# A two-layer decode kernel: norms in two products, queries turned in PSUM, the gate worked ahead, one more V head kept, K slots freed by halves

## The chip, the cores and the metric

The kernel runs on one core of a Trainium2 chip. Its time is the device time of one execution in microseconds (us), the median of several runs. Smaller is better.

## The reference, cut to what matters

Four sequences (B = 4) decode one token each. The same block, attention and then a gated feed-forward net, is applied twice with the same weights and the same K and V caches:

```python
B, Sq, D = 4, 1, 512;  Hq, Hkv, Sk, Dh = 32, 8, 4096, 128;  F = 1792   # all bf16
x = x + _A_ref(_layernorm(x), A_k_cache, A_v_cache, A_wq, A_wo)
x = x + _B_ref(_layernorm(x), B_w_gate, B_w_up, B_w_down)
x = x + _A_ref(_layernorm(x), A_k_cache, A_v_cache, A_wq, A_wo)
x = x + _B_ref(_layernorm(x), B_w_gate, B_w_up, B_w_down)
# _A_ref: q = x @ wq;  softmax(q k^T / sqrt(128)) v, 4 query heads to a K/V head;  @ wo
# _B_ref: (gelu(x @ w_gate) * (x @ w_up)) @ w_down
```

One head of K or V of one sequence is 4096 x 128 bf16, 1 MiB; the whole K cache is 32 MiB, the V cache 32 MiB, and the weights are 13.25 MiB. The kernel keeps twelve head-sized slots beside the weights; what is not kept for the second pass is read twice.

## The kernel before, in words

**Tiling and stages.** Below, L is the pass: 0 for the first application of attention, 1 for the second. Sequences are taken one after the other. For sequence b the kernel loads its 8 K heads and keeps them for both passes, computes the scores of pass 0, streams the V heads of pass 0, goes through the dense chain (output projection, norm, feed-forward, norm, query projection), computes the scores of pass 1 on the K heads still there, and streams the V heads again for pass 1. The pass-1 V loads of sequence b come after the K and pass-0 V loads of sequence b + 1. At the end one output projection, norm and feed-forward for all four sequences, and the output.

**Slots.** `KV` has 12 slots of 1 MiB (`SLOTS`); the four quarters of `wq_sb` serve as four more once the last query projection is done (`extra`, line 994). A slot has two halves, and a load takes a slot (`ld_head`, line 348, issued on line 351) or, for the V loads named in `HALVES`, half a slot (`ld_part`, line 354, issued on line 357). V head 7 of sequences 1, 2 and 3 is loaded once and kept for pass 1 (`HELD`); that of sequence 0 is loaded twice. A K head gives both halves of its slot free when the pass-1 scores of its group of four heads are complete (`loads_k`, line 753).

**Loads.** All loads go through SyncE's queue in one fixed order (`pl.load`, lines 804 to 818): x, wq, K of sequence 0, half of wo, V, the other half of wo, the gate, up and down weights (the down weights in two loads of 7 chunks, line 798), then K(1), V(1) pass 0, V(0) pass 1, K(2), and so on. A load that waits for its slot holds up all loads behind it.

**Order of the other work.** `Plan` (line 64) holds a node for each step with an assumed duration; `run` (line 108) goes through them with assumed costs and priorities (`LEAD`, `PATIENCE`) and writes down one order, in which each engine then executes. `warm` (line 215) puts spare matmuls, whose results nobody reads, into TensorE's planned gaps (`spin`, line 1002, executed on line 1004).

**Scores.** `scores(b, z, m)` (line 401): group z of four K heads, half m of each head's keys, 16 matmuls of 512 columns (line 415). K heads other than 5 and 7 are first transposed in place by VectorE in two halves (`turn`, line 363, executed on line 366); heads 5 and 7 go through TensorE (line 373) and ScalarE (line 379).

**The dense chain.** `outproj` (line 878): the first groups of heads with `proj` (line 613), out of PSUM in two halves (line 632), summed by a matmul (line 639), the last groups straight to their place with `proj_last` (line 623); then `addback` (transpose on line 646, add on line 647). `ln` (line 821): square (line 500), one product with ones for sums and squares together (line 506), reduction and centring (lines 512 and 513), variance (lines 521 and 522), and ScalarE's root (lines 529 and 530) beside what follows. The feed-forward: gate and up products (`up`, line 655), the gate's transpose (`ffturn`, line 662), the polynomial of gelu (lines 678 to 681), the exponential on ScalarE (line 688), then the up product's transpose (line 662 again), its product with the gate (lines 695 to 699), division (lines 705 to 707), and the down product in two steps (line 715). `qproj` (line 829): for each half z of the query heads 16 matmuls (line 538), ScalarE takes them out of PSUM (line 551), VectorE transposes (line 556), `qsplit` masks (line 595), a small matmul (line 605) and `expand` (line 392) spread the queries for the scores.

**The end.** After the last V half: scale (line 493), `proj_last`, `addback`, the rows of x for the residual (lines 727 and 728), norm, feed-forward, sum (line 732), output (line 735).

## Time and profile before

| | |
|---|---|
| median of 3 runs | 292.3 us (291.77 to 293.2) |
| the profiled execution's own time | 291.89 us |
| its span in the profile | 290.1 us |
| time around the span (start and end) | 1.8 us |
| granted TensorE clock | 0.998 |
| loads: K 32 of 1 MiB; V 38 of 1 MiB (4 of them into `wq_sb`) and 46 of 512 KiB | 93 MiB |
| read from HBM | 111.42 MB |

In the profile, PE is TensorE's matmul, PEld its weight load, DVE VectorE, ACT ScalarE, SP SyncE with the loads' queue. "L351" is line 351 of the kernel. A line of the chain of waits or of the timeline begins with its start and its length in us. In a table by stretches the columns are the stretch, its length, the busy time and count of each engine, the granted clock, the busy share of the 16 DMA engines (it can read over 1), and the GB/s moved.

### The profile page before, as it was taken

How to read it: one execution, taken by the hardware profiler on the slowest of the kernel's cores; microseconds unless marked ns; L12 is line 12 of the kernel's file. 1: busy time of each engine (PE TensorE's matmuls, PEld its weight loads, DVE VectorE, ACT ScalarE, POOL GpSimd, SP SyncE). 2: the span in 40 equal slices, each digit the busy share in tenths (PEclk: the TensorE clock that was granted, in tenths of full speed). 3: DMA queues.
4: the chain of work that ended last, by engine and by line, in shares of the span. 5: the costliest groups of instructions: out<-in, count | busy, mean ns of one | idle time of the engine just before them, and what ended most of it. 6: DMA issues, size and time to landing. Idle time of an engine off the chain costs nothing.

```text
span 290.1 us, 9733 instructions
## 1 busy us (share of the span) xinstructions
PE 236.3 (81%) x4419; PEld 138.3 (48%) x4419; DVE 133.5 (46%) x380; ACT 74.5 (26%) x167; POOL 0.7 (0%) x6
## 2 busy tenths in 40 slices
PE   4988887878687888798888698879977889897794
PEld 1433454443233565455434465554445655565552
DVE  4149911002289942052389721343998213444034
ACT  1020751001023852101224731000338321113010
POOL 0000000000000000000000000000000000000000
PEclk9999999999999999999999999999999999999999
DMA  7999999999999999999999999999999999999910
GB/s 312 412 421 419 376 405 416 414 371 426 415 407 395 419 421 417 402 407 406 393 417 416 425 416 411 405 407 390 413 422 416 408 387 403 396 382 420 411 47 1
DMA packets 21657, 112.04 MB, mean 386 GB/s; under 512 B 2032, under 2 KB 6128, under 8 KB 12272
## 3 DMA queue, kind: packets, MB, share of 16 engines
q1 hardware_dynamic: 21568, 111.42, 95.3%
q8 instruction: 34, 0.56, 0.8%
q14 instruction: 7, 0.06, 0.0%
q10 hardware_dynamic: 48, 0.01, 0.0%
HBM read 111.42 MB, written 0.00 MB: 384 GB/s over the span
## 4 chain that ended last, share of the span: by engine, by line
DMA 62%; PE 16%; SPq 11%; DVE 7%; issue 2%; ACT 1%; DVEq 0%
DMA KV<-in_A_v_cache_dram 43%; DMA KV<-in_A_k_cache_dram 8%; SPq L351 7%; PE O_ps L485 7%; DMA wd_sb<-in_B_w_down_dram 6%; DMA wq_sb<-in_A_v_cache_dram 5%; SPq L741 3%; PE S_ps L415 3%; DVE KV L366 2%; PE R_ps L715 1%; PE R_ps L538 1%; DVE PA L662 1%; PE S_ps L1004 1%; PE R_ps L655 1%; DVE sm L421 1%
## 5 line engine op out<-in xcount | busy, mean ns | idle before, releaser
L485 PE MATMUL O_ps<-PA,KV 128*128 128x56 bf16 x1920 | 66.3, 188 | 20.8 <-DMA KV<-in_A_v_cache_dram 17.3
L485 PEld LDWEIGHTS <-KV 128*128 128x128 bf16 x1920 | 57.6, 97 | 40.8 <-DMA KV<-in_A_v_cache_dram 32.4
L1004 PE MATMUL S_ps<-iden_b 128*128 128x512 bf16 x226 | 67.7, 401 | 3.6 <-DVE iden_b L321 3.6
L366 DVE STREAM_TRANSPOSE KV<-KV 128x1024 int32<-128x1024 int32 x48 | 56.5, 1214 | 0.6 <-DMA KV<-in_A_k_cache_dram 0.4
L379 ACT ACTIVATE KV<-R_ps 128x512 bf16<-128x512 f32 x64 | 34.9, 595 | 28.0 <-PE R_ps L373 27.9
L415 PE MATMUL S_ps<-KV,PA 128*32 128x512 bf16 x384 | 35.3, 394 | 2.1 <-DVE KV L366 1.3
L1004 PEld LDWEIGHTS <-iden_b 128*128 128x128 bf16 x227 | 21.9, 107 | 27.6 <-issue 11.7
L373 PE MATMUL R_ps<-iden_b,KV 128*128 128x128 bf16 x256 | 22.1, 219 | 6.3 <-ACT KV L379 3.1
L421 DVE TENSOR_REDUCE sm<-S_ps 128x1 f32<-128x512 f32 x16 | 10.8, 677 | 27.4 <-PE S_ps L415 27.4
L373 PEld LDWEIGHTS <-KV 128*128 128x128 bf16 x256 | 15.8, 97 | 14.8 <-issue 10.2
L415 PEld LDWEIGHTS <-PA 128*32 128x32 bf16 x384 | 11.4, 94 | 13.2 <-issue 4.4
L493 DVE TENSOR_TENSOR OT<-O_ps,XS 128x4 bf16<-128x4 f32 (+1 forms) x12 | 2.0, 164 | 32.9 <-PE O_ps L485 32.9
L415 PE MATMUL S_ps<-KV,QN 128*32 128x512 bf16 x128 | 16.8, 381 | 0.2 <-ACT KV L379 0.2
L438 ACT ACTIVATE PA<-S_ps,sm 128x512 bf16<-128x512 f32 x16 | 11.7, 732 | 20.4 <-DVE sm L432 17.6
L632 ACT ACTIVATE PA<-R_ps 128x256 f32<-128x256 f32 x10 | 3.8, 384 | 46.2 <-PE R_ps L613 41.1
L529 ACT ACTIVATE sm<-sm 128x1 f32<-128x1 f32 (+1 forms) x10 | 2.0, 203 | 52.6 <-DVE sm L522 52.6
L493 DVE TENSOR_TENSOR OT<-O_ps,rdk 128x16 bf16<-128x16 f32 (+3 forms) x18 | 3.1, 170 | 26.7 <-PE O_ps L485 26.7
L463 ACT ACTIVATE PA<-T_ps 128x512 bf16<-128x512 f32 x16 | 9.6, 597 | 13.0 <-PE T_ps L455 11.8
L556 DVE STREAM_TRANSPOSE PA<-PA 128x256 int32<-128x256 int32 x10 | 4.4, 437 | 14.9 <-ACT PA L551 14.2
L613 PE MATMUL R_ps<-wo_sb,OT 128*1 128x512 bf16 (+1 forms) x124 | 8.7, 378 | 2.6 <-DMA wo_sb<-in_A_wo_dram 1.4
L646 DVE STREAM_TRANSPOSE PA<-R_ps 128x128 f32<-128x128 f32 x9 | 2.9, 317 | 16.5 <-PE R_ps L623 10.2
L447 DVE STREAM_TRANSPOSE PA<-PA 128x256 int32<-128x256 int32 x16 | 7.0, 434 | 7.5 <-ACT PA L438 7.5
(92 smaller groups left out, 173.9 us busy)
## 6 DMA issues: line engine op xcount, KB each, us to landing
KV<-in_A_v_cache_dram SPq DMA_DIRECT2D x34, 1024.0 KB, 15.0
KV<-in_A_k_cache_dram SPq DMA_DIRECT2D x32, 1024.0 KB, 13.5
KV<-in_A_v_cache_dram SPq DMA_DIRECT2D x46, 512.0 KB, 7.0
wq_sb<-in_A_wq_dram SPq DMA_DIRECT2D x1, 4096.0 KB, 12.2
wo_sb<-in_A_wo_dram SPq DMA_DIRECT2D x2, 2048.0 KB, 19.5
wq_sb<-in_A_v_cache_dram SPq DMA_DIRECT2D x4, 1024.0 KB
wg_sb<-in_B_w_gate_dram SPq DMA_DIRECT2D x1, 1792.0 KB
wu_sb<-in_B_w_up_dram SPq DMA_DIRECT2D x1, 1792.0 KB
```

The lines of the kernel that those rows point to most:

```text
L351: nc.sync.dma_start(out=where[name], in_=src.rearrange("(p c) d -> p (c d)", p=P))
L366: nc.vector.transpose(out=w, in_=w)
L373: nc.tensor.matmul(R_ps[k % 2][:, P * u:P * u + P], lhsT=where[name][:, at:at + P], rhs=iden_b[:], start=True, stop=True)
L379: nc.scalar.activation(out=where[name][:, 512 * k:512 * k + 512], in_=R_ps[k % 2][:], func=ACT.Copy)
L415: nc.tensor.matmul(S_ps[z][32 * t:32 * t + 32], lhsT=w, rhs=k, start=(m == 0 and x == 0), stop=(m == 1 and x == 3))
L421: nc.vector.tensor_reduce(out=cms[:, z:z + 1], in_=S_ps[z][:].rearrange("p c r -> p (c r)"), axis=AX.X, op=ALU.max)
L438: nc.scalar.activation(out=PW[L][z].rearrange("p (a r e) -> p a r e", a=8, e=2), in_=S_ps[z][:].rearrange("p (a e) r -> p a r e", e=2), fu ...
L463: nc.scalar.activation(out=PW[L][z], in_=T_ps[z][:].rearrange("p t x -> p (t x)"), func=ACT.Copy)
L485: nc.tensor.matmul(Ov[L][:, j], lhsT=vw[:, c, :], rhs=w[:, c // 2, :, c % 2].unsqueeze(1).broadcast_to([P, WIDE, 4]), start=(m == 0 and c ...
L613: nc.tensor.matmul(R_ps[0][32 * i:32 * i + nb, :], lhsT=src[:, 4 * j + i, 0:nb], rhs=wo_sb[:, 4 * j + i, :], start=(first and j == heads[0 ...
L741: return lambda pick: nc.sync.dma_start(out=dst, in_=src.rearrange(pat, q=P))
L1004: nc.tensor.matmul(sinks[place].rearrange("p (a n) -> p a n", a=4), lhsT=iden_b[:], rhs=every, start=True, stop=True)
```

## The change

- The sums and the squares of a norm become two products. The first no longer waits for the squares; the second goes to another PSUM place and feeds only the variance.
- For the first half of the query heads of the dense chains (not for the first query projection), the 16 matmuls leave the queries in an order in which VectorE transposes them within PSUM; ScalarE's way out is gone there. The second half stays.
- In the feed-forward the gate's branch (exponential, division) is worked through before the up product is transposed. That transpose and the last product are cut in two (8 and 6 chunks), the down weights' loads and the down product likewise. At the end, the rows' transpose for the residual goes behind the norm.
- V head 7 of sequence 0 is kept for pass 1 too; its two half loads go.
- A K slot is given free in two halves, each after its own half of the pass-1 scores. K head 3 of sequence 1 comes in two loads of half a slot, the second into the other half of the first one's slot.
- In the last projection heads 4 and 5 are scaled and projected apart.
- The planner's assumed durations and priorities change (`LEAD`, `PATIENCE`, `WARM`, `FILL`, the sizes given to `pl.load`), and with them the order on each engine. The spare matmuls go from 227 to 263.

```diff
-HELD = ((), (7,), (7,), (7,))
-HALVES = {(b, 1, j) for b in range(3) for j in range(8)} | {(3, 1, 6)}
+HELD = ((7,), (7,), (7,), (7,))
+HALVES = {(b, 1, j) for b in range(3) for j in range(7)} | {(3, 1, 6)}
+HALF_HELD = (None, None, None, None)
+K_HALVES = {(1, 3)}
...
-DMA_FETCH = 1.5
+DMA_FETCH = 0.8
...
-WARM = 0.45
-FILL = 0.7
+WARM = 0.55
+FILL = 0.9
...
+    CUT = (0, 8, CF)
...
+    def ln_place(s, nb):
+        return O_ps[0][:, 512 - CD * nb:] if s else R_ps[1][:, 0:CD * nb]
+
-    def ln_mm(bs, nb):
+    def ln_mm(s, bs, nb):
         def emit():
-            st = R_ps[1][:, 0:2 * CD * nb].rearrange("p (s k b) -> p s k b", s=2, k=CD)
-            nc.tensor.matmul(st, lhsT=ones_mean, rhs=XS[:, :, :, bs], start=True, stop=True)
+            st = ln_place(s, nb).rearrange("p (k b) -> p k b", k=CD)
+            nc.tensor.matmul(st, lhsT=ones_mean, rhs=XS[:, s, :, bs], start=True, stop=True)
...
+    def qmm_apart(bs):
+        def emit():
+            for c in range(CD):
+                w = wq_sb[:, c, :].rearrange("q (z g h j k e) -> q z g h j e k", z=2, g=2, h=8, j=2, e=2)
+                for jg in range(4):
+                    nc.tensor.matmul(R_ps[0][32 * jg:32 * jg + 1, :].rearrange("p (h e k) -> p h e k", h=8, e=2),
+                                     lhsT=xn[:, c, bs], rhs=w[:, 0, jg % 2, :, jg // 2],
+                                     start=(c == 0), stop=(c == CD - 1))
+        return emit
+
+    def qturn_apart():
+        nc.vector.transpose(out=R_ps[0][:], in_=R_ps[0][:])
...
-            pl.load(("k", b, j), 8, ld_head(("k", b, j), A_k_cache[b, j]), [("sc", b, 1, j // 4, 1)],
-                    soft=soft)
+            name, src = ("k", b, j), A_k_cache[b, j]
+            rd = [[("sc", b, 1, j // 4, m)] for m in range(2)]
+            if (b, j) in K_HALVES:
+                for m in range(2):
+                    if j >= 3:
+                        soft = [("sc", b - 1, 1, 0 if j < 7 else 1, m)]
+                    pl.load(name + (m,), 4.15, ld_part(name, m, src), rd[m], soft=soft, half=True)
+            else:
+                pl.load(name, 8, ld_head(name, src), rd, soft=soft)
...
     def ln(tag, after, bs, nb, y, by=1.0):
-        a = add(("lnq", tag), "DVE", 0.17, [after], ln_sq(bs, nb))
-        a = add(("lnm", tag), "PE", 0.4, [a], ln_mm(bs, nb), ins=4)
-        a = add(("lnc", tag), "DVE", 0.37, [a], ln_mid(bs, nb))
-        v = add(("lnv", tag), "DVE", 0.33, [a], ln_var(nb))
+        s = add(("lnq", tag), "DVE", 0.17, [after], ln_sq(bs, nb))
+        m = add(("lnm", tag), "PE", 0.35, [after], ln_mm(0, bs, nb), ins=4)
+        a = add(("lnc", tag), "DVE", 0.3, [m], ln_mid(bs, nb))
+        s = add(("lns", tag), "PE", 0.35, [s, m], ln_mm(1, bs, nb), ins=4)
+        v = add(("lnv", tag), "DVE", 0.45, [s, a], ln_var(nb))
...
+            if not z and not root:
+                after = add(("qm", tag, z), "PE", 1.1, [after], qmm_apart(bs), ins=32)
+                last = add(("qt", tag, z), "DVE", 0.72, [after], qturn_apart)
+                last = spread_q(b, 1, z, last, "apart")
+                continue
...
+    def ffn(tag, a, bs, nb, y, clear=None):
+        one = nb == 1
+        g = [None, None]
+        for z, w in ((0, wg_sb), (1, wu_sb)):
+            g[z] = add(("up", tag, z), "PE", 0.93, [a, g[0], "wu" if z else "wg"], up(z, w, bs, nb), ins=32)
+        t0 = add(("ft", tag, 0), "DVE", 0.65, [g[0]], ffturn(0))
+        a = add(("ga", tag), "DVE", 0.59 if one else 0.72, [t0, ("lnr", ("f", tag))], gelu_a(nb, y))
+        e = add(("gb", tag), "ACT", 0.22 if one else 0.25, [a], gelu_b(nb))
+        if not one:
+            a = add(("gz", tag), "DVE", 0.28, [a], gelu_z(nb, y))
+        e = add(("gd", tag), "DVE", 0.72 if one else 0.95, [e, a], gelu_d(nb, y))
+        t1, h, n = a, None, None
+        for k in range(2):
+            t1 = add(("ft", tag, 1 + k), "DVE", (0.44, 0.36)[k], [g[1], t1], ffturn(1, k))
+            h = add(("gh", tag, k), "DVE", 0.18, [t1, e, h], gelu_h(nb, k))
+            if k and clear:
+                add(("zz", tag), "DVE", 0.07, [h], clear)
+            n = add(("dn", tag, k), "PE", (0.55, 0.42)[k], [h, n, ("wd", k)], down(nb, k), ins=8 * (CUT[k + 1] - CUT[k]))
+        return n
```

More of the change, by code (lines that the diff above doesn't have):

```diff
@@ L607, in qrep, with proj @@
         return emit
-    def proj(src, nb, heads, first, last):
+    def proj(src, cols, nb, heads, first, last):
         def emit():
@@ L616, in proj, with proj_last @@
         return emit
-    def proj_last(src, nb, heads, last):
+    def proj_last(src, cols, nb, heads, last):
         def emit():
@@ L876, in parts, with outproj @@
         return [(h, [("os", b, 1, i)]) for i, h in enumerate(g)]
-    def outproj(tag, b, L, bs, nb, after):
-        pre, p = None, parts(b, L)
-        whole = len(p) - (1 if L else 2)
+    def outproj(tag, p, whole, L, bs, nb, after, free):
+        pre, cols = None, bs if L else slice(0, 1)
         for k, (heads, deps) in enumerate(p[:whole]):
             pre = add(tag + (k,), "PE", 0.21 * len(heads) + 0.15, deps + [pre] + after,
-                      proj(OT[L], nb, heads, k == 0, k == whole - 1), ins=8 * len(heads))
-        free = [("val", b, 0, j, 1) for j in range(4)]
+                      proj(OT[L], cols, nb, heads, k == 0, k == whole - 1), ins=8 * len(heads))
         for m in range(2):
```

169 lines of the change are left out of this document (84 added, 85 removed).

## The prediction

> **What bounds the kernel now.** I read the page's second, third and fourth parts first, then tables by stretches.
>
> ```profile
> span 290.1 us, 9733 instructions
> DMA  7999999999999999999999999999999999999910
> q1 hardware_dynamic: 21568, 111.42, 95.3%
> DMA 62%; PE 16%; SPq 11%; DVE 7%; issue 2%; ACT 1%; DVEq 0%
> ```
>
> The transfers are busy from the first slices to the last but two. 111.42 MB leave in one queue, and 62% of the chain that ended last is DMA. So bytes set the time, together with the moments in which the queue has nothing to do, and the end, where no transfer is left. The stretches give the speed and those moments; the last column is GB/s.
>
> ```profile
> 84.00:90.00 6.00, 4.93 (x84) 2.52 (x87) 5.57 (x15) 1.49 (x5) 0.00 (x0) 1.00 0.93 377
> 100.00:110.00 10.00, 8.31 (x180) 6.06 (x178) 4.59 (x9) 5.82 (x12) 0.00 (x0) 1.00 1.02 419
> 120.00:130.00 10.00, 9.22 (x228) 5.95 (x227) 4.14 (x19) 1.00 (x4) 0.00 (x0) 1.00 1.02 405
> 140.00:146.00 6.00, 4.97 (x99) 2.62 (x97) 3.35 (x9) 1.53 (x4) 0.00 (x0) 1.00 0.99 385
> 196.00:202.00 6.00, 5.51 (x117) 3.14 (x113) 1.33 (x4) 0.60 (x1) 0.00 (x0) 1.00 1.02 387
> 230.00:236.00 6.00, 5.27 (x128) 3.54 (x120) 2.16 (x8) 1.38 (x3) 0.00 (x0) 1.00 0.98 380
> 248.00:258.00 10.00, 8.57 (x207) 5.00 (x207) 3.27 (x17) 1.60 (x4) 0.00 (x0) 1.00 1.02 372
> ```
>
> Whole-slot loads run at 419 GB/s (100 to 110), half-slot loads at 405 (120 to 130). Against 419, the stretch 84 to 90 loses (419 - 377) / 419 x 6 = 0.60 us; the four later ones lose 0.49, 0.46, 0.56 and 1.12, together 2.63. These are the places where loads wait for slots.
>
> **The change, part by part.**
>
> *One MiB less: -2.5.* V head 7 of sequence 0 isn't loaded again. 1.0486 MB at 405 GB/s are 2.59 us; K head 3 of sequence 1, loaded by halves now, goes from 2.50 (at 419) to 2.59. The net is -2.50.
>
> At this place the Trainium skill speaks against the split: "DMA: Bandwidth & Descriptors", sections on the anatomy of one DMA and on bandwidth, gives each DMA a fixed 2.0 us beside its bytes and asks for at least 1 MiB. By it, an estimate, K head 3 in two loads costs 2.0 us more than in one, and the sum would be -1.1. The 405 against 419 disagrees with that for loads in a filled queue.
>
> *The slot that the kept head holds: +1.1.* After the down weights, the queue has had the first four K heads of sequence 1 in the slots that V of pass 0 left; the rest wait for the pass-1 scores to free K slots. The kept head leaves three such slots. The chain of waits, and the timeline, show how far the scores are:
>
> ```profile
> 61.10 17.76 DMA wd_sb<-in_B_w_down_dram
> 78.90 0.59 PE R_ps L715 x28
> 80.07 0.18 DVE XS L500
> 80.29 0.40 PE R_ps L506 x2
> 81.16 1.04 PE R_ps L538 x16
> 82.22 0.61 ACT PA L551
> 82.85 0.46 DVE PA L556
> 83.33 0.27 DVE qs L595
> ```
>
> ```profile
> 81.38 1.25 DVE L366 STREAM_TRANSPOSE KV<-KV 128x1024 int32<-128x1024 int32 x1
> 84.39 2.02 PE L415 MATMUL S_ps<-KV,PA 128*32 128x512 bf16 x32 [0.21 <-DVE PA L392]
> 86.42 3.08 SPq L351 DMA_DIRECT2D KV<-in_A_k_cache_dram  x4
> ```
>
> The weights land at 78.86, and the next K load goes out at 86.42, right behind the 32 score matmuls. With three heads the queue is empty 2.50 us sooner. Against that, the first half of a slot is free after 16 of the 32, 1.0 sooner. The chain itself: 24 instead of 28 down matmuls save 4/28 x 0.59 = 0.08, the square (80.07 to 80.29) leaves the path, 0.22, and ScalarE's way out with the transpose behind it (82.22 to 83.31, 1.09) gives place to one transpose in PSUM.
>
> That transpose is new. Between the rows that are nearest, from PSUM:
>
> ```profile
> L662 DVE STREAM_TRANSPOSE PA<-R_ps 128x448 f32<-128x448 f32 x10 | 6.5, 648 | 7.2 <-PE R_ps L655 7.1
> L646 DVE STREAM_TRANSPOSE PA<-R_ps 128x128 f32<-128x128 f32 x9 | 2.9, 317 | 16.5 <-PE R_ps L623 10.2 <-PE R_ps L715 6.3
> L333 DVE MEMSET O_ps<- 128x512 f32 x2 | 1.0, 485 | 0.1
> ```
>
> a column costs (648 - 317) / 320 = 1.03 ns, so 512 cost 0.71 us. The floor is 0.65 (the 448-column row); the ceiling, with all of a 512-column PSUM write on top, 1.20. I take 0.71, for the shape and the source are the same. That would gain 0.38. But in the changed order of VectorE's instructions a K head's transpose of 1.25 (line 366, from 81.38 before) now stands directly ahead of it, and ends at about 82.6. The query turn then ends at 82.6 + 0.71 = 83.3, where it ended before: the chain of sequence 0 gains nothing. So the first half slot is asked for 1.0 sooner and the queue is empty 2.50 sooner. If all engines ran dry together, this would add 1.5; in 84 to 90 the queue still moved 377 of 419, so they run dry one by one. I take +1.1, between 0.3 (the last engine hardly waits) and 2.5 (the halves don't help).
>
> *The chains of sequences 1 to 3: -1.3.* There the square and the query turn do gain, 0.22 twice and 0.38, for no K transpose stands before them; and the new order puts the chain ahead: the pass-1 scores of group 0 stand before the last V head's two halves, where they stood between and behind them. In the chain of waits before:
>
> ```profile
> 140.77 0.60 PE O_ps L485 x16
> 141.38 1.13 PE S_ps L415 x16
> ```
>
> the last V half's 16 matmuls come first and the scores end at 142.5; this is in the stretch that loses 0.49. The K load that is third in the queue now goes into a K slot freed by these scores. Of the 2.63 us lost in the four later stretches I take back half, 1.3: most of the first two (0.95), whose place this is, a third of the others. The bounds are -2.6 (all) and 0.
>
> *The end: -0.4.* From the timeline of the last 12 us:
>
> ```profile
> 278.41 0.39 PE L639 MATMUL R_ps<-PA,sm 128*4 128x128 f32 x4
> 278.73 0.61 PE L485 MATMUL O_ps<-PA,KV 128*128 128x56 bf16 x16
> 280.68 0.17 DVE L500 TENSOR_TENSOR XS<-XS 128x16 f32<-128x16 f32 x1
> 280.90 0.41 PE L506 MATMUL R_ps<-XS,sm 128*128 128x32 f32 x2 [0.59 <-DVE XS L500]
> 280.97 0.41 DVE L728 STREAM_TRANSPOSE PA<-PA 128x128 f32<-128x128 f32 x1
> 284.05 0.22 DVE L681 SCALAR_TENSOR_TENSOR PA<-PA 128x56 f32<-128x56 f32 x1
> 284.30 0.25 ACT L688 ACTIVATE PA<-PA 128x56 f32<-128x56 f32 x1 [1.80 <-DVE PA L681]
> 285.31 0.50 DVE L706 RECIPROCAL PA<-PA 128x56 f32<-128x56 f32 x1
> 286.12 0.95 PE L715 MATMUL R_ps<-wd_sb,PA 128*4 128x128 bf16 x56 [1.01 <-DVE PA L707]
> 287.12 0.29 DVE L732 TENSOR_TENSOR PA<-PA,R_ps 128x128 bf16<-128x128 f32 x1 [1.06 <-PE R_ps L715]
> 287.48 0.68 SPq L735 DMA_DIRECT2D out_dram<-PA  x2
> ```
>
> The last V half's product waits at 278.73 behind a sum of line 639, which the new order puts earlier: -0.2, between 0 and the sum's 0.39. The norm's product starts at 280.68 instead of 280.90: -0.22. The rows' transpose of 0.41 moves to the wait for the gate product (0.96), which hides it; without that cover it would cost its 0.41. The gate's branch gains nothing here, worked through from the gelu's end (284.26): a multiplication 0.24, eight chunks' transpose 0.45 by the slope above, sum and minimum 0.12, reciprocal 0.52, product 0.23, product 0.2, then 32 matmuls beside six chunks' transpose 0.38 and a product 0.2, then 24 matmuls, 0.42: 2.8, as from 284.26 to 287.07 before. Bounds for the end: -0.9 (the second transpose wholly hidden) and 0.
>
> *At nothing:* 36 more spare matmuls (they stand in gaps), the strided query weights (the scores' matmuls of line 415 read their K heads strided too, 16 in 1.13 us as line 538 has 16 in 1.04), and the masked queries read from PSUM, under 0.1 in a chain that isn't at the end. If a gap is shorter than planned, a spare matmul of 0.22 delays what stands behind it, and the V halves with it; that is in the third rival.
>
> *Sum:* -2.5 + 1.1 - 1.3 - 0.4 = -3.1. The profiled execution (291.89, of which 1.8 lie around the span) would come to 288.8; it lies 0.4 below the median of the runs shown, and the forecast for the median is 292.3 - 3.1 = **289.2**.
>
> **The rivals.**
>
> 1. *The gap takes the MiB.* For it: VectorE's K transpose ahead of the query turn. If the first half slot goes out no sooner than 86.42, the whole 2.5 is lost after 84, and if the chains then win nothing either, the end alone is left: 292.3 - 0.4 = 291.9. Against it: half a slot is free after 16 of 32 score matmuls, whatever the chain does. 0.14.
> 2. *All the lost time comes back.* -2.6 instead of -1.3, +0.3 instead of +1.1, -0.9 at the end: 292.3 - 5.7 = 286.6. For it: the stretches lose only while loads wait. Against it: in 120 to 130 loads by halves move 405 with no wait in sight. 0.12.
> 3. *The chain blocks the V halves (slower).* TensorE works in order. With norm, query product (0.41 + 0.4 + 1.04 = 1.9 us) and scores ahead of V halves that have landed, their half slots are given back that much later. If three chains each cost 1.9, the time is 292.3 - 2.5 + 1.1 + 5.7 - 0.4 = 296.2. It decides by more than 0.5% from (1.46 + 2.5 - 1.1 + 0.4) / 3 = 1.1 us each. For it: 248 to 258 before, where chain and halves mix, is the worst stretch, 1.12. Against it: three slots of halves are 7.8 us of transfers in hand. 0.09.
> 4. *A small load into an empty queue pays its way alone.* From the output's issue (287.48) to the span's end (290.1) there are 2.6 us for 1 KB; one such way more, at the gap, gives 289.2 + 2.6 = 291.8. The skill's fixed 2.0 says the same with its own figure. Against it: 405 against 419. 0.02.
>
> **How the numbers follow.** The forecast's own case, 288.0 to 290.8, has 0.63; the rivals 0.14, 0.12, 0.09 and 0.02. A measurement of this kernel tells about 0.5% from no change, 1.46 us: faster is below 290.84, slower above 293.76. Faster: 0.63 + 0.12 = 0.75. Same: 0.14 + 0.02 = 0.16. Slower: 0.09. From 287.0 to 291.9 the range leaves out the slower case and about half of the second rival, some 0.15 to 0.17.
>
> **What would show it.** The queue's bytes fall by 1.05 MB. The stretch 84 to 90 moves less than 377 GB/s, with the first half-slot K load at about 85.5; a load at 84.7 would say that the K transpose wasn't in the way, one at 86.4 the first rival. The dips around 140 and 196 (moved by what was won until then) rise towards 405; if they are deeper, the third rival is at work. At the end, the norm's product follows the add-back at once, and from the gelu's end to the last matmul it is still 2.8 us. The forecast is wrong if the gap costs over 2 us or if the V halves' products wait for TensorE and not for DMA.

## The result, and the profile after

The changed kernel takes 295.1 us (292.43 to 295.79, 7 runs) beside 292.8 us (median of 7) of the kernel before on the same chip: ratio 1.0068, 95% interval 1.0038 to 1.0097. It is 0.68% slower, 2.0 us, where 289.2 us, 3.1 less than before, was forecast. All times below are compared as ratios to the kernel before, measured beside each kernel on the same chip. A ratio is formed from the executions in the faster of two states alone (one of before, 298.56 us, was in the slower), so it isn't the quotient of the medians. The profiled execution took 295.61 us, 0.5 above its median, with a span of 293.8. That is 3.7 above the span of before, more than the ratio's 2.0: part of what the two traces differ in is the spread between executions.

The page of the changed kernel, the lines that answer to those of before:

```profile
span 293.8 us, 9878 instructions
PEclk9999999999999999999997999999999999979999
DMA  7999999999979999999999999999999999999800
q1 hardware_dynamic: 21424, 110.37, 93.8%
DMA 45%; PE 32%; DVE 9%; ACT 5%; SPq 4%; issue 4%; DVEq 0%; ACTq 0%
```

The bytes fell by 1.05 MB as they should, and yet DMA's share of the chain fell from 62% to 45%: TensorE's rose from 16% to 32%, "issue" from 2% to 4%. The kernel was a stream of loads with TensorE beside it; in this execution the two take turns in setting the time. The clock row has a 7 in two places; by the trace these are two windows of 3.4 us at half speed, at 154.9 and 257.3. The profiled execution of before had none ahead of its last 1.1 us, but the kernel before isn't free of them: its other executions have mean granted clocks of 0.968 to 1.0.

The same seven stretches as before (last column GB/s):

```profile
84.00:90.00 6.00, 5.27 (x91) 2.88 (x90) 5.24 (x13) 1.25 (x4) 0.00 (x0) 1.00 0.66 221
100.00:110.00 10.00, 7.23 (x149) 5.35 (x147) 5.63 (x12) 6.75 (x14) 0.00 (x0) 1.00 1.01 418
120.00:130.00 10.00, 8.77 (x213) 5.63 (x213) 2.76 (x15) 1.17 (x4) 0.00 (x0) 1.00 1.01 402
140.00:146.00 6.00, 5.53 (x107) 2.81 (x106) 2.60 (x11) 1.42 (x4) 0.00 (x0) 1.00 1.00 378
196.00:202.00 6.00, 5.30 (x134) 3.63 (x134) 1.12 (x2) 0.00 (x0) 0.00 (x0) 1.00 0.97 337
230.00:236.00 6.00, 5.86 (x133) 3.78 (x132) 2.15 (x8) 2.10 (x5) 0.00 (x0) 1.00 1.01 414
248.00:258.00 10.00, 7.43 (x202) 5.40 (x201) 4.96 (x23) 0.81 (x2) 0.00 (x0) 0.96 1.01 384
```

The speeds of loads in a filled queue (418, 402) are unchanged. 84 to 90 fell from 377 to 221: (419 - 221) / 419 x 6 = 2.84 us lost, 2.24 more than before. 196 to 202 fell from 387 to 337, 0.72 more. 230 to 236 is the one that rose clearly (380 to 414). By the trace's transfers the last load ends at 280.0 instead of 278.0, and from there to the end of the span it is 13.8 us instead of 12.1. Of the 3.7 us of span, 2.0 are lost while loads run and 1.7 behind them.

The gap, in the timeline of the changed kernel (start, length; in brackets the idle time ahead and who ended it):

```profile
81.78 1.25 DVE L373 STREAM_TRANSPOSE KV<-KV 128x1024 int32<-128x1024 int32 x1 [0.23 <-DMA KV<-in_A_k_cache_dram]
82.94 0.69 DVE L569 STREAM_TRANSPOSE R_ps<-R_ps 128x512 f32<-128x512 f32 x1
84.69 2.06 PE L422 MATMUL S_ps<-KV,PA 128*32 128x512 bf16 x32 [0.18 <-DVE PA L399]
85.84 1.27 SPq L364 DMA_DIRECT2D KV<-in_A_k_cache_dram  x2
87.21 2.67 SPq L358 DMA_DIRECT2D KV<-in_A_k_cache_dram  x4
```

The K head's transpose stands ahead of the query turn, as forecast, and the first half-slot load goes out at 85.84 (forecast 85.5), behind the first 16 score matmuls. Its first bytes move at 86.79, 0.95 us after the issue; the queue has run dry by then, and from 86.3 to 86.8 no transfer engine moves anything.

Three rows of the chain of waits are new in kind:

```profile
194.97 1.37 issue
...
253.81 2.44 issue
...
273.95 1.45 issue
```

In these TensorE stands still in the middle of a group of matmuls and waits for nothing that the profile shows. The second is followed by the half-speed window at 257.3, the third lies on the chain of waits, which from there to the end holds no load: the last V half's product starts at 282.41, 2.4 us behind the last transfer, where before it was 278.73, 0.7 behind.

The end itself, from the last add-back on:

```profile
283.78 0.32 DVE L676 STREAM_TRANSPOSE PA<-R_ps 128x128 f32<-128x128 f32 x1 [0.44 <-PE R_ps L653]
284.36 0.39 PE L516 MATMUL R_ps<-XS,sm 128*128 128x16 f32 x2 [0.17 <-DVE XS L677]
285.45 0.41 DVE L767 STREAM_TRANSPOSE PA<-PA 128x128 f32<-128x128 f32 x1
287.47 0.22 DVE L713 SCALAR_TENSOR_TENSOR PA<-PA 128x56 f32<-128x56 f32 x1
289.44 1.02 PE L752 MATMUL R_ps<-wd_sb,PA 128*4 128x128 bf16 x56 [0.47 <-DVE PA L744]
290.51 0.29 DVE L771 TENSOR_TENSOR PA<-PA,R_ps 128x128 bf16<-128x128 f32 x1 [0.61 <-PE R_ps L752]
```

From the last V half's product to the end of the residual's sum it is 290.80 - 282.41 = 8.39 us; before, 287.41 - 278.73 = 8.68. So the end gained 0.29. From the gelu's end (287.69) to the last matmul's (290.46) it is 2.77, as before (2.81).

### The profile page after: what moved, and what is told of

Same layout as the page of the kernel before. It is cut to its first block, busy times and chain, and to the rows that moved or that the text cites. A ratio compares the mean times of both kernels' runs of the same rounds, so it can differ in the third digit from the quotient of the medians.

```text
span 293.8 us, 9878 instructions
## 1 busy us (share of the span) xinstructions
PE 244.8 (83%) x4487; PEld 145.8 (50%) x4487; DVE 135.9 (46%) x401; ACT 71.7 (24%) x163; POOL 0.7 (0%) x6
## 4 chain that ended last, share of the span: by engine, by line
DMA 45%; PE 32%; DVE 9%; ACT 5%; SPq 4%; issue 4%; DVEq 0%; ACTq 0%
DMA KV<-in_A_v_cache_dram 30%; DMA KV<-in_A_k_cache_dram 13%; PE O_ps L492 11%; PE S_ps L1059 6%; PE S_ps L422 6%; DVE KV L373 3%; SPq L780 3%; ACT KV L386 2%; DMA PA<-in_A_x_dram 2%; PE R_ps L752 1%; PE R_ps L685 1%; ACT PA L445 1%; PE R_ps L380 1%; PE R_ps L552 1%; PE R_ps L563 1%
## 5 line engine op out<-in xcount | busy, mean ns | idle before, releaser
L492 PEld LDWEIGHTS <-KV 128*128 128x128 bf16 x1920 | 58.5, 97 | 32.8 <-DMA KV<-in_A_v_cache_dram 16.9
L1059 PE MATMUL S_ps<-iden_b 128*128 128x512 bf16 x259 | 71.2, 397 | 3.6 <-DVE iden_b L328 3.6
L1059 PEld LDWEIGHTS <-iden_b 128*128 128x128 bf16 x263 | 24.8, 105 | 30.6 <-issue 9.3
L422 PE MATMUL S_ps<-KV,PA 128*32 128x512 bf16 x384 | 36.4, 417 | 0.6 <-DVE PA L399 0.5
L380 PEld LDWEIGHTS <-KV 128*128 128x128 bf16 x256 | 15.9, 97 | 15.4 <-issue 8.9
L422 PEld LDWEIGHTS <-PA 128*32 128x32 bf16 x384 | 12.5, 100 | 9.8 <-issue 4.3
L422 PE MATMUL S_ps<-KV,QN 128*32 128x512 bf16 x128 | 15.9, 380 | 0.2 <-ACT KV L386 0.2
L500 DVE TENSOR_TENSOR OT<-O_ps,rdk 128x4 bf16<-128x4 f32 (+2 forms) x19 | 3.3, 174 | 22.7 <-PE O_ps L492 22.7
L470 ACT ACTIVATE PA<-T_ps 128x512 bf16<-128x512 f32 x16 | 9.5, 597 | 16.1 <-PE T_ps L462 13.8
L475 PE MATMUL S_ps<-mask_th,sm 128*128 128x16 f32 x32 | 6.1, 266 | 6.8 <-ACT PA L445 6.4
L475 PEld LDWEIGHTS S_ps<-mask_th,sm 128*128 128x128 f32 x32 | 4.9, 187 | 12.1 <-ACT PA L445 12.1
L694 DVE STREAM_TRANSPOSE PA<-R_ps 128x448 f32<-128x448 f32 (+2 forms) x15 | 7.4, 491 | 5.8 <-PE R_ps L685 5.8
## 6 DMA issues: line engine op xcount, KB each, us to landing
KV<-in_A_v_cache_dram SPq DMA_DIRECT2D x35, 1024.0 KB, 13.8
```

Source lines behind the costliest of these rows:

```text
L380: nc.tensor.matmul(R_ps[k % 2][:, P * u:P * u + P], lhsT=where[name][:, at:at + P], rhs=iden_b[:], start=True, stop=True)
L422: nc.tensor.matmul(S_ps[z][32 * t:32 * t + 32], lhsT=w, rhs=k, start=(m == 0 and x == 0), stop=(m == 1 and x == 3))
L470: nc.scalar.activation(out=PW[L][z], in_=T_ps[z][:].rearrange("p t x -> p (t x)"), func=ACT.Copy)
L475: nc.tensor.matmul(S_ps[z][:, 0, 0:16], lhsT=sms[:, z:z + 1].broadcast_to([P, P]), rhs=mask_th[:].rearrange("p t h -> p (t h)"), start=Tru ...
L492: nc.tensor.matmul(Ov[L][:, j], lhsT=vw[:, c, :], rhs=w[:, c // 2, :, c % 2].unsqueeze(1).broadcast_to([P, WIDE, 4]), start=(m == 0 and c ...
L1059: nc.tensor.matmul(sinks[place].rearrange("p (a n) -> p a n", a=4), lhsT=iden_b[:], rhs=every, start=True, stop=True)
```

## The experiments

Two theories stood at the start. **Gap**: the kept head empties the queue at 84 to 92 and this eats the MiB. **Bunching**: the new order crowds TensorE's work, it runs out of instructions ("issue"), the clock falls, and V halves are given back late. Their rivals: the split of K head 3, the clock alone, the edited steps themselves. Ratios are to the kernel before beside them; for scale, 0.34% are 1.0 us.

**1. The spare matmuls left out.** In the changed kernel, order kept:

```diff
-                k = max(int(min(most, ...
+                k = 0
```

> The changed kernel with its order kept and all 263 spare matmuls left out. They write sums that nobody reads, so the result is the same. Theory F (TensorE runs out of instructions where much work stands close together, which is the idle time called issue, 1.37 us at 195 and 2.44 us at 253.8): 526 instructions fewer, so these two stalls shrink below 0.7 us each. Theory C (the half-speed windows of 3.4 us at 154.9 and 257.3 follow idle TensorE): far more half-speed windows, a mean granted clock under 0.9, and a time over 298 us. Theory G (the loss is the empty queue at 84 to 92): that stretch stays at about 249 GB/s. If C is small and F large: about 292 us.

297.58 us, ratio 1.0143 (1.0103 to 1.0183), slower than the change by 0.75%. Its page, and its waits of TensorE (sum, count, longest):

```profile
PEclk9985988855558699999955998899758999998897
```

```profile
PE O_ps L491 <- issue: 0.7, 1, 0.7
```

The unexplained idle time is down to 1.8 us in all (the changed kernel has 4.3 and 2.4 in its two groups, 6.7), but the clock is at half speed for 30 us around 75, and 84 to 92 moves 129 GB/s. So the spare matmuls earn more than they cost here. That the idle time goes by the number of instructions doesn't follow from this: with the same 263 spare matmuls in the same order it is 3.6 us in experiment 2 and 2.2 in experiment 16.

**2. K head 3 in one load.** Order kept; the one load stands where the second half stood:

```diff
+            if name == ("k", 1, 3, 0):
+                continue
+            if name == ("k", 1, 3, 1):
+                e, pick = ld_head(("k", 1, 3), A_k_cache[1, 3]), (pick[0], 0)
```

> The changed kernel, same order, but K head 3 of sequence 1 comes in one load of a whole slot at the place of its second half load (issued when both halves of the slot are free, about 0.9 us after the first half load was). Theory G1 (the queue is empty because the kept head left a MiB less to load; the split helps by 0.9 us): 84 to 92 falls below 249 GB/s, time 0.5 to 1 us more. Theory G2 (the 4 KB rows of the half loads are slow in coming into an empty queue, which is why 88 to 91 moves so little): 84 to 92 rises to 270 or more, time 0.5 to 1.5 us less.

293.69 us, ratio 1.0034 (1.0006 to 1.0063): 0.34% of 0.68% come back by undoing the split. Each ratio has an error of about 0.3%, so this pair alone doesn't decide; two more follow (experiments 3 and 8, 9 and 10). The place was not the one I had in mind: 84 to 92 moves 258 GB/s instead of 249, 0.2 us. What changes is when the K heads behind are there. In the chain of waits, the load of K head 5 and what waits for it (start, length), first the changed kernel, then this one:

```profile
87.68 9.76 DMA KV<-in_A_k_cache_dram
97.49 0.41 PE R_ps L380 x4
```

```profile
87.46 8.89 DMA KV<-in_A_k_cache_dram
...
96.39 0.41 PE R_ps L380 x4
```

1.1 us of difference, though the queue had moved only 0.3 us less by then. The trace's landings tell why. A load is shared out over 16 transfer engines, and lands with the last of them. The second half load of K head 3 landed on the first engine at 90.12 and on the last at 92.44, a spread of 2.3 us; K heads 4 and 5 behind it spread over 1.95 and 1.9. With the whole load the spread is 0.4 for all three. In the kernel before, whose queue isn't empty there, K heads 3 to 5 spread over 1.6 to 1.7. So behind the gap whole loads land in step, here three of them (the next, K head 6, spreads over 1.7 again), and that is a gain. Of the two half loads the first is in step as well (88.49 to 88.95); the spread begins with the second. TensorE works in order, so its scores then run 1.0 to 1.1 late: 100.44 against 99.35, 138.36 against 137.40. By 144 the queue has lost that as well:

```profile
130.00:150.00 20.00, 18.02 (x379) 10.83 (x378) 9.83 (x35) 2.85 (x9) 0.00 (x0) 1.00 1.01 392
```

```profile
130.00:150.00 20.00, 18.32 (x367) 10.84 (x366) 10.80 (x34) 2.63 (x8) 0.00 (x0) 1.00 1.02 411
```

Changed kernel first: 392 against 411 GB/s, 19 / 419 x 20 = 0.9 us. In the seven kernels of this order that have spare matmuls, a late K head 5 mostly goes with a slow stretch: landings at 95.94 and 96.35 with 412 and 411 GB/s, at 97.44 to 99.34 with 383 to 396. Experiment 16 is the exception (97.75, with 405). So the way from the spread to the loss fits the traces, and isn't shown beyond that. The Trainium skill says in "DMA: Bandwidth & Descriptors", section on two DMAs through the same engine, that nothing orders transfers across the 16 engines; the spread agrees with that.

**3. The query turn ahead of the K transpose.** The changed kernel with that transpose of VectorE put behind the spread of the queries:

```diff
+    late = [o for o in order if o[0] == ("tn", 1, 0, 0)]
+    order = [o for o in order if o[0] != ("tn", 1, 0, 0)]
+    at = [n for n, _ in order].index(("qx", 0, 1, 0)) + 1
+    order[at:at] = late
```

> The changed kernel, same order but for one instruction: the transpose of the first half of K head 0 of sequence 1, 1.25 us, stands behind the spreading of the queries of sequence 0 instead of ahead of the query turn in PSUM. Theory G: the scores start about 0.9 us sooner, the first half-slot load goes out at about 84.9 instead of 85.84, 84 to 92 gains 0.9 us (from 249 to about 290 GB/s), and the time falls by 0.5 to 0.9 us. Rival (the loads' way into an empty queue sets the stretch): the load goes out sooner, the stretch gains less than 0.3 us.

295.33 us, ratio 1.0087 (1.0052 to 1.0122). 84 to 92 rises only to 267 GB/s; the time doesn't follow. The order of these two was not the point.

**4. The V head not kept, K loads whole**, all else as changed, planned anew:

```diff
-HELD = ((7,), (7,), (7,), (7,))
-HALVES = {(b, 1, j) for b in range(3) for j in range(7)} | {(3, 1, 6)}
+HELD = ((), (7,), (7,), (7,))
+HALVES = {(b, 1, j) for b in range(3) for j in range(8)} | {(3, 1, 6)}
...
-K_HALVES = {(1, 3)}
+K_HALVES = set()
```

> The changed kernel without the two edits on slots of sequence 0: V head 7 is loaded twice again and K head 3 in one load; the planner makes its order anew. Bytes rise by 1.05 MB to 111.42. Theory G (the kept head costs 2.7 us at 84 to 92 and saves 2.5): the stretch goes back to 370 to 380 GB/s and the time stays within 1 us of the changed kernel's, 294 to 296. Theory F or C (fetch or clock are the loss): also near the changed kernel's, with stalls called issue and half-speed windows still there. If neither (the chains' edits do gain): 291 or below.

294.14 us, ratio 1.0035 (1.0003 to 1.0066). 84 to 92 is back at 358, 138 to 146 at 416, and the time is still 0.35% above before, just clear of its error: a third loss, about 1.0 us, lies neither in the gap nor in the split. Beside experiment 2, which has the kept head and also a whole K head 3, this tells what the kept head is worth with the new code: 1.0034 with it, 1.0035 without it.

**5. The V head kept, nothing else**, in the kernel before, planned anew:

```diff
-HELD = ((), (7,), (7,), (7,))
-HALVES = {(b, 1, j) for b in range(3) for j in range(8)} | {(3, 1, 6)}
+HELD = ((7,), (7,), (7,), (7,))
+HALVES = {(b, 1, j) for b in range(3) for j in range(7)} | {(3, 1, 6)}
```

> The kernel before with one edit: V head 7 of sequence 0 is kept (a K slot is still freed whole, K head 3 loaded whole, old chains; the planner orders anew). 1.05 MB fewer. Theory G (the kept head's slot empties the queue): the stretch 84 to 92 falls from 385 to about 260 to 290 GB/s, 2 to 2.5 us lost there, and the time is that of the kernel before within 0.7 us. Rival (the kept head is worth its bytes, and the changed kernel loses by its order alone): 290 to 291.

292.7 us, ratio 0.9987 (0.9957 to 1.0017).

```profile
84.00:92.00 8.00, 6.92 (x117) 3.59 (x114) 7.32 (x16) 2.15 (x5) 0.00 (x0) 1.00 0.65 249
86.50:87.50 1.00, 1.00 (x23) 0.64 (x20) 0.97 (x2) 0.18 (x1) 0.00 (x0) 1.00 0.00 0
```

Before:

```profile
84.00:92.00 8.00, 6.93 (x114) 3.64 (x114) 7.57 (x16) 1.99 (x6) 0.00 (x0) 1.00 0.95 385
```

The gap nearly by itself (the new plan has 6 more spare matmuls in its trace, and little else moves): 249 GB/s where before had 385, (385 - 249) / 419 x 8 = 2.6 us, for 2.5 us of bytes. From 86.5 to 87.5 nothing moves at all. The theory of the gap holds: keeping the head is worth nothing that can be measured here. K heads 3 to 5 land with a spread of 0.4 us, 96.41 for K head 5 against 97.07 in the kernel before, although the queue has moved 2.6 us less; that may be why the gap didn't cost more than it did.

**6 and 7. The priorities of before**, with the changed code planned anew: once with the bytes of before, once with the kept head and K whole.

```diff
-DMA_FETCH = 0.8
-PATIENCE = (0.4, 1.5, 0.6)
-LEAD = {"tn1": -3, "val0": 0, ...
-WARM = 0.55
-FILL = 0.9
+DMA_FETCH = 1.5
+PATIENCE = (0.5, 1.5, 0.7)
+LEAD = {"tn1": -3, "val0": 1, ...
+WARM = 0.45
+FILL = 0.7
```

> The changed kernel's code (norms in two products, queries turned in PSUM, gate ahead, K slots by halves) without the kept head and the split K head, planned with the priorities and costs of the kernel before: 211 spare matmuls, the chains later among the V halves. Theory F (the new order packs TensorE's instructions closer than they arrive): the issue stalls over 1 us around 254 go or shrink, 248 to 258 rises from 349 to 370 or more, and the time is at or under the kernel before, 291.5 to 292.9. Rival (the code edits themselves cost): it stays at 294.

> As the one before it, but V head 7 of sequence 0 is kept, K head 3 still in one load. Theory G: 84 to 92 at about 260 GB/s, and a time within 0.7 us of the kernel without the kept head. Rival (a MiB less shows): 1.5 to 2.5 us less than that.

295.24 us, ratio 1.0059 (1.002 to 1.0098), and 293.57, ratio 1.0027 (1.0003 to 1.0051). Neither gives the order of before back, for the assumed durations differ; each gives an order of its own. The two differ by 0.3%, within their errors. They say no more than that an order can be worth some tenths of a per cent.

**8. Two and three together**, K whole and the query turn ahead:

> The changed kernel in its own order with K head 3 whole and the K transpose behind the query turn, both at once. Theory G: the first K load after the gap goes out about 0.9 us sooner than with the whole load alone, the time falls by 0.3 to 0.9 us from its 293.7. Theory F: the end still trails, the issue stall near 254 stays at 1.5 to 2.4 us, so the time stays over 292.5.

293.68 us, ratio 1.0028 (0.9998 to 1.0057). Beside experiment 3, this is a second pair with and without the split: 0.59%. K head 3's second half spreads over 2.9 us there, the whole load over 0.4 here, and 130 to 150 moves 412 instead of 390 GB/s (in experiment 3 a half-speed window at 137.6 has a part in that).

**9 and 10. Half of the spare matmuls** (156 instead of 263), with the split and with K whole:

```diff
-                spin(*idle[name])
+                spin(idle[name][0], (idle[name][1] + 1) // 2)
```

> The changed kernel in its own order, with 156 spare matmuls instead of 263 (each group of k spares cut to half of k, rounded up); what they compute is read by nobody. Supply of instructions as the cause: of the 6.7 us in which TensorE waited for nothing but its next instruction before the V products and the second query product, under 3 are left (with none of the spares 0.7 were), the stretch 194 to 204 rises from 336 GB/s towards 390, and the time falls by 0.7 to 1.5 us, to about 294. Clock as the cause: more windows of half speed than the two of the changed kernel, granted clock below 0.95, and the time rises towards the 297.6 of the kernel without spares. Neither: 295.1 within 0.5.

> The same with K head 3 of sequence 1 loaded whole: 156 spare matmuls. Supply: from 293.7 to about 292.5 to 293, the 1.5 us before the second query product gone. Clock: above 294.5 with a granted clock below 0.95. The two loads of half a slot as a cost of their own: this one lies 1.4 below the kernel with half the spares and both half loads, as 293.7 lies below 295.1.

296.06 us, ratio 1.0124 (1.0086 to 1.0163), and 294.73, ratio 1.0048 (1.0015 to 1.0081). The waits of the first:

```profile
PE O_ps L492 <- issue: 2.5, 4, 1.0
```

6.7 us of unexplained idle time became 2.5, and the time rose; the granted clock fell from 0.988 to 0.943. Idle time and clock change together in this kernel, so it doesn't tell what the idle time costs by itself; fewer spare matmuls are no way to be rid of it at a profit. The third pair gives the split 0.76%, and 130 to 150 moves 383 and 396 GB/s. In experiment 10 only the first whole load lands in step (0.4); K heads 4 and 5 spread over 1.7 all the same, and K head 5 is there 0.5 us sooner than in experiment 9 (98.82 against 99.34).

**11. The shorter steps alone**, in the exact order of before: norm in two products, query turn in PSUM, the rows behind the last norm.

```diff
...
+        pl.nodes["qm", b, 0]["emit"] = qmm_apart(slice(b, b + 1))
+        pl.nodes["qe", b, 0]["emit"] = lambda: None
+        pl.nodes["qt", b, 0]["emit"] = qturn_apart
+        pl.nodes["qs", b, 1, 0]["emit"] = qsplit(0, "apart")
...
+    order.insert(at.index(("lnv", "f2")) + 1, turned)
```

> The kernel before with its own order, loads and spare matmuls; only the shorter steps are put into it: every norm in two products, the first half of the queries turned in PSUM, and the rows' transpose of the end behind the last norm. My forecast of the chains and of the end, if shortening by itself pays: a good part of 1.3 + 0.3 us, 291.5. If the chain is no bound in those stretches (loads, not the chain, end last): the end's 0.2 to 0.3 alone, 292.8 beside 293.0. If bunched work on TensorE is what costs: 293.5 to 294.5, with idle time before an instruction that nothing else explains above the 2.7 us of before.

292.21 us, ratio 0.9999 (0.9979 to 1.0019).

```profile
138.00:146.00 8.00, 7.05 (x135) 3.64 (x134) 3.73 (x11) 1.53 (x4) 0.00 (x0) 1.00 1.01 394
194.00:204.00 10.00, 8.86 (x186) 5.18 (x182) 3.77 (x15) 1.19 (x4) 0.00 (x0) 1.00 1.00 387
```

Before has 394 in both. The shorter chains win nothing in the stretches in which I expected most of the 1.3 us, and the whole, the end's gain included, is 0 within 0.6 us.

**12. Half of the spare matmuls in the kernel before** (150 instead of 227), the same edit as in 9:

> The kernel before with 150 spare matmuls instead of 227 (each group cut to half, rounded up). Supply: 2.7 us of such idle time go, and the time falls by up to 0.7, to 292.3. Clock: windows of half speed appear and the time rises by 1 or more, to 294 or more. If both are small, 293 within 0.5; then what costs in the changed kernel is not the number of its spares.

294.0 us, ratio 1.0041 (1.0002 to 1.0081), just clear of its error; clock 0.947 in the profiled execution. Also here fewer spares cost. One stretch says something else:

```profile
248.00:258.00 10.00, 8.45 (x215) 5.46 (x214) 4.03 (x19) 1.82 (x5) 0.00 (x0) 1.00 1.03 400
```

The profiled execution of before has 372 there. No step is changed here, nor the order, so the 1.12 us that I had counted as lost in this stretch needn't be a wait for the chain; experiment 11 has 402 and can't claim it for its shorter steps.

**13 and 14. The gate ahead too, then the kept head too**, still planned with the durations and priorities of before:

```diff
...
+    def products(nb):
+        def emit():
+            for k in range(2):
+                ffturn(1, k)()
+                gelu_h(nb, k)()
+        return emit
```

> The kernel before in its own order, with the shorter steps (norm in two products, query turn in PSUM) and, new here, the gate's branch worked ahead of the up product's transpose, that transpose and the down product in 8 and 6 chunks. Loads, slots and spare matmuls are those of before. If the steps themselves cost the 1.3 us by which the changed kernel with the bytes of before (294.1) lies above it: about 294. If they cost nothing and the planner's order does: 292.2 to 292.8, within 0.3% of before.

> The same with V head 7 of sequence 0 kept: the whole change but the half K loads, the slots freed by halves and the new order. Gap as measured so far: 1.05 MB less, and 84 to 92 down to about 250 GB/s, so 292.3 to 293, the same as the kernel without the kept head within 0.7. If it is this and the whole K load at 293.7 differs from it, the order carries the rest; if it comes out at 293.7 too, the order carries nothing.

293.99 us, ratio 1.0041 (1.0012 to 1.007), and 293.27, ratio 1.0016 (0.9989 to 1.0043). Whether the gate's rework costs something stays open: the first says 0.4%, the second, with the same rework, is within the error of before. The first one's 84 to 92 moves 343 GB/s, where experiment 11 has 379; the rest is near before. It was profiled at its median (293.97 us) with a full clock (1.00), so the clock isn't what this execution lost by.

**15. The new priorities alone**, in the kernel before: only the five constants of experiment 6, the other way round.

> The kernel before with nothing but the changed kernel's priorities (the constants of the planner, those for spare matmuls among them), planned anew: another order, 287 spare matmuls. Order as the cause of the rest: 293.5 or more, over 0.3% slower, with losses in 138 to 146, 194 to 204 or 248 to 258 above those of before. If an order made for other durations is as good here: 292.5 within 0.5.

295.95 us, ratio 1.0088 (1.0053 to 1.0123). No step, no byte and no slot differs from before; the order, and 287 spare matmuls instead of 227, do.

```profile
138.00:146.00 8.00, 7.42 (x156) 4.54 (x156) 3.31 (x13) 1.64 (x4) 0.00 (x0) 1.00 0.99 375
194.00:204.00 10.00, 8.37 (x193) 5.38 (x189) 3.44 (x12) 2.24 (x5) 0.00 (x0) 1.00 0.99 376
248.00:258.00 10.00, 8.63 (x243) 5.88 (x237) 5.19 (x22) 1.93 (x6) 0.00 (x0) 1.00 1.02 399
```

Before, for the same three stretches:

```profile
138.00:146.00 8.00, 6.76 (x133) 3.65 (x134) 3.53 (x10) 1.53 (x4) 0.00 (x0) 1.00 1.00 394
194.00:204.00 10.00, 8.61 (x181) 4.95 (x177) 3.68 (x14) 2.01 (x5) 0.00 (x0) 1.00 1.03 394
248.00:258.00 10.00, 8.57 (x207) 5.00 (x207) 3.27 (x17) 1.60 (x4) 0.00 (x0) 1.00 1.02 372
```

This costs as much as the whole change. But the trace can't show where: the profiled execution, 293.4 us, was the fastest of eight, the others took 294.3 to 296.6. In it 138 to 146 loses 0.36 us more than before, 194 to 204 loses 0.43 more, and 84 to 92 is at 349 instead of 385. The rise at 248 to 258 needn't be the order's: experiment 12 has it too. The clock alone isn't the cause. It was full in the profiled execution and 0.983 to 0.994 in the others; but at the same granted clock of 0.983 to 0.988 the kernel before took 293.6 us (median of 9) on this chip, and this one 296.1 (median of 5). And the order isn't the changed kernel's own, which is planned with other durations. So this run shows that an order can cost 2.6 us, not how it does so.

**16. Both half loads together**, when the whole slot is free:

```diff
+            if name == ("k", 1, 3, 0):
+                first = e, pick
+                continue
+            if name == ("k", 1, 3, 1):
+                e(pick)
+                e, pick = first
```

> The changed kernel with the two half loads of K head 3 issued one behind the other when the whole slot is free, the second half first. In the trace of the changed kernel the second half load lands over 2.3 us from the first transfer engine to the last (0.4 us for whole loads), and all loads behind it keep that spread; so K head 5 is there 1.1 us later and TensorE waits for it. If a lone half load with a wait behind it makes the spread: under 1 us of spread here, and 293.7 as with the whole load. If loads of half size make it, wherever they are: the spread stays, and 295 too. If neither the spread nor the split is the cause: 295 with a small spread.

294.64 us, ratio 1.006 (1.0027 to 1.0094). The half load that is issued second spreads over 0.4 us (90.92 to 91.31), so the 2.3 of the changed kernel aren't due to the size of a load alone. But K heads 4 and 5 spread over 1.3 again, K head 5 is there at 97.75 only, and the gap is deeper:

```profile
84.00:92.00 8.00, 7.11 (x117) 3.87 (x117) 7.09 (x20) 1.97 (x6) 0.00 (x0) 1.00 0.63 224
```

224 against 258 with one whole load is 0.65 us. So the split loses in this form too, partly in another way; by time it can't be told from the changed kernel. The theory of bunching can be checked here:

```profile
PE O_ps L492 <- issue: 2.2, 3, 1.3
```

This is all the unexplained idle time of this kernel, less than the 2.7 us of before, in an execution at the median. So a loss of nearly this size comes without the standstills of the changed kernel (6.7 us). For the clock, 0.983 in this execution, the run decides nothing.

## Why the prediction was wrong, point by point

*One MiB less, -2.5: right.* 1.05 MB less, at unchanged speeds of 418 and 402 GB/s.

*The slot that the kept head holds, +1.1: the term that was mis-sized.* The kept head alone lowers 84 to 92 by 2.6 us and leaves the time at 0.9987. The upper bound of 2.5 was the value, and the net of -1.4 that I gave the kept head (-2.5 + 1.1) is about 0: four pairs with and without it (experiment 5; 2 and 4; 7 and 6; 14 and 13) give it 0.13, 0.01, 0.32 and 0.25%, 0.0 to 0.9 us, none clear of its error. The step that failed is the conclusion that the engines, since they run dry one by one, hardly wait. In experiment 5 none of them moves anything from 86.5 to 87.5: the K load goes out at 86.67, and its first bytes move only at 87.62. These 0.95 us from issue to bytes stand nowhere in my sum; before, some 11 of the 16 engines still had work at 87.0. My own sign of being wrong, a gap that costs over 2 us, came true. I had also argued that half a slot comes 1.0 sooner. The first half load did go out at 85.84, but with the two half loads the 16 engines came out of step, and what the first won at 86 to 88 (213 GB/s against 57 with a whole load) was lost again by 92 (225 against 336, then 332 against 418). This is the first rival's mechanism, which had 0.14, though not by its condition (a load no sooner than 86.42).

*The split of a K load, costed at 0.09: wrong.* It costs 0.34%, 0.59% and 0.76% in three pairs, 1.0 to 2.2 us; the first of them isn't clear of its error, the other two are. The figure that the Trainium skill gives for one more DMA (2.0 us, in a section on loads that GpSimd issues; here SyncE issues them) lies in this span, but where that is a fixed time of each load, the trace shows a spread over the transfer engines, behind which the next loads land late. My answer to it, 405 against 419, came from a filled queue; this load goes into an empty one. I had that case before me as the fourth rival, and gave it 0.02.

*The query turn, 0.71 us: right.* The group of all four:

```profile
L569 DVE STREAM_TRANSPOSE R_ps<-R_ps 128x512 f32<-128x512 f32 x4 | 2.9, 721 | 2.9 <-PE R_ps L563 2.9
```

721 ns. That the chain of sequence 0 gains nothing was right too: its scores start at 84.69, before at 84.39.

*The chains of sequences 1 to 3, -1.3: failed.* Shortened steps in the old order give 0.9999, 0 within 0.6 us: what waits in those stretches isn't waiting for the chain. And the new order, which I counted as a gain, isn't one: experiment 4 has it with the new code and is 0.35% slower, and the new priorities alone make the kernel before 0.88% slower. My third rival had the slower side, at 0.09, by V halves blocked behind the chain and deeper dips around 140 and 196. That mechanism isn't shown. The dips are there in the changed kernel (376 GB/s in 138 to 146, 336 in 194 to 204), but in experiment 2, in the same order, they are gone (413 and 394).

*36 more spare matmuls at nothing: not refuted.* Halving the spares costs 0.56%, 0.14% and 0.41% in three kernels, leaving all out 0.75%; more of them were not tried alone.

*The end, -0.4: mechanism right,* 0.29 measured, 0.2 of it from the norm's product, which follows the add-back at once. The rows' transpose of 0.41 (285.45) lies under the gate product as forecast, and the gate's branch takes 2.8 as before. In the profiled execution it is outweighed by TensorE, which is 1.7 us further behind the loads when the end begins.

From the kernel before to the changed one the experiments make three steps: the new code in its new order +1.0 us (experiment 4), the kept head 0.0 (experiment 2), the split +1.0 (the changed kernel). They come to the measured 2.0 by construction, and each has an error of about 1 us. Against the forecast of -3.1 this is a miss of 5.1: 1.5 at the slot of the kept head, 1.3 at the chains, and the rest in the split and the order, which had no price or next to none. In all kernels planned by new durations or new priorities the ratio is 1.0027 or more; of the four planned as before, with the edits put in, two are at 0.9987 and 0.9999 (kept head; shorter steps) and two, with the gate ahead, at 1.0041 and 1.0016. None beats the kernel before by more than its error.

Open: why the second half load leaves the engines out of step; how an order costs time, and how much of the 1.0 us of the new code in its new order is the order's; whether the gate ahead costs.

## What to carry to other kernels

A head kept on chip saves bytes only where its slot isn't the one that feeds the queue in its next gap: count the time that the queue stands empty at its full price first, the way from issue to first bytes included, then the bytes. Keep an edit to the steps apart from an edit to the planner's constants, and measure each: here a new order cost more than any step won. Be wary of splitting a load where the queue is empty, and read landings by their last engine, not by bytes. Before you read a cause off a trace, look where its execution lies among the others.

## What the runs showed of the hardware

- A load lands with its last of 16 engines. Of two half loads into an empty queue, each issued when its half came free, the first spread over 0.4 to 0.6 us and the second over 2.3 (2.8 to 4.1 in experiments 1, 3 and 9), and the loads behind it over 1.9 or more. Issued together (experiment 16), both were in step, and the next load had 1.3. Whole loads into the same empty queue spread over 0.3 to 0.4, the first three or four of them in five kernels, the first alone in a sixth (experiment 10). Where the queue hadn't run quite dry, the first load spread over 0.3 to 1.8. Ahead of the gap all kernels have 1.7 to 2.4. So an empty queue puts the engines back in step, but not for long.
- From the issue of a load into an empty queue to its first bytes it took 0.95 us (85.84 to 86.79 in the changed kernel, 86.67 to 87.62 in experiment 5).
- TensorE stood still for up to 2.44 us inside a group of 16 matmuls of one form, with loads at 384 GB/s beside it. The sum of these times is 2.2 to 6.7 us in three kernels with 263 spare matmuls, 2.5 and 3.2 in two with 156, and 1.8 with none. What makes them wasn't shown. If they were instructions fetched late, "Runtime: NRT & Kernel Launch" of the Trainium skill, section on instruction fetch mechanics, would speak against it: it has fetches hidden.
- The clock falls to half speed in windows of 3.4 us (in experiment 1 also in multiples of it, up to 30.7). In the changed kernel one follows the longest standstill, and 32 score matmuls take 3.03 us instead of 2.06:

```profile
256.25 1.02 PE L552 MATMUL R_ps<-wq_sb,xn 128*1 128x512 bf16 x13 [2.44 <-issue]
258.49 3.03 PE L422 MATMUL S_ps<-KV,PA 128*32 128x512 bf16 x32
```

"TensorE: Matmul & The Clock Gate" of the Trainium skill, Part 1, gives windows of 3413 ns and half the clock; the trace agrees.
